# A hash-masked attention followed by an MLP: fp16 transposes, exponentials as the stationary side, and the MLP of one batch woven into the attention of the next

## Chip, cores, metric

The kernel runs on one core of a Trainium2 chip. The metric is the device time of one execution in microseconds (us), the median of several runs. All runs that are compared here are fast (within 1.5% of the fastest run of the same kernel) unless a sentence says otherwise; where some runs of a kernel counted as slow, the median given is that of the fast ones and their number is said. Times inside a kernel come from the trace of one profiled execution, whose span is about 2 us shorter than the device time.

A ratio given with an interval is the mean time of one kernel's fast runs over the mean time of the other kernel's fast runs of the same rounds, so it is not quite the ratio of the medians that are quoted next to it. The experiments ran on four different chips; on each the kernel before took between 423.1 and 423.9 us in the median, so the ratios to it can be compared across chips.

## The reference

Four batches of 8 heads, 768 positions, head dimension 64. Each query and key gets a 6-bit hash (signs of a projection); a query attends only to keys of the same hash. The heads are put side by side (512 columns), and each token goes through an MLP with 2048 hidden units and the activation h cos(h).

```python
q_bits = (np.einsum('bhsd,dk->bhsk', q, proj) > 0)          # k likewise
mask = q_bucket[:, :, :, None] == k_bucket[:, :, None, :]
scores = scale * np.matmul(q, k.transpose(0, 1, 3, 2))
scores = np.where(mask, scores, -1000000000.0)
attn = softmax(scores)                                        # shortened here
x = np.matmul(attn, v).transpose(0, 2, 1, 3).reshape(3072, 512)
h = x @ w_in                                                  # 512 x 2048
out = (h * np.cos(h)) @ w_out                                 # 2048 x 512
```

## The kernel before

Both kernels use the same trick for the mask: the six bits, as +0.5 or -0.5, are appended to the 64 rows of q and k, so that one matmul of 70 rows gives score plus a large bonus for equal hashes, and the exponential of anything else is practically zero. All heads are done first, then all of the MLP. For one head (cuts marked with `...`):

```python
# q and k side by side, [128 positions, 128]: fp32 transposes on TensorE
for t in range(SB):
    nc.tensor.matmul(out=psum_t[:, t*P:(t+1)*P], lhsT=qk_nat[:, t, :], rhs=ident,
                     is_transpose=True, ...)                              # L142
nc.vector.tensor_copy(out=qk_f32, in_=psum_t)                             # L151
for c0, c1 in ((0, 512), (512, 768)):                                     # the hash, fp32
    nc.tensor.matmul(out=psum_t[0:38, c0:c1], lhsT=projx2, rhs=qk_f32[:, c0:c1], ...)  # L159
nc.vector.tensor_scalar(out=q_ext[D:KEXT, :], in0=psum_t[0:NBITS, :], ...)             # L166
...
for jt in range(SB):                                      # 6 steps of 128 keys
    # scores transposed: keys on the partitions, 768 queries along the row
    nc.tensor.matmul(out=st_ps[:, c0:c1], lhsT=k_ext[:, jt*P:(jt+1)*P],
                     rhs=q_ext[:, c0:c1], ...)            # L221, 512 and 256 columns
    nc.scalar.activation(out=pt_sb[:, 0:S], in_=st_ps, func=Exp, ...)     # L229
    # V (and 64 columns of ones) stationary, the exponentials move
    nc.tensor.matmul(out=out_ps[:, c0:c1], lhsT=v_ext[:, jt, :],
                     rhs=pt_sb[:, c0:c1], ...)            # L210, 512 and 257 columns
nc.vector.tensor_scalar(out=numpair[b][t][r0:r0+D, :], in0=out_ps[0:D, 0:S], ...)      # L267
nc.scalar.copy(out=denpair[b][t][r0:r0+D, :], in_=out_ps[D:P, 0:S])                    # L271
```

After the last head each batch is normalised (logarithm and exponential of the denominators on ScalarE, L292 and L298, product on VectorE, L304), and the MLP runs in six chunks of 512 tokens: L321 is the first layer, L329 the sine, L337 the product, L353 and L364 the second layer.

The softmax here doesn't subtract the row's maximum and nothing guards it: scores larger than these inputs give would overflow.

## Time and profile before

| | before |
|---|---|
| time, median | 422.88 us |
| start to first steady score | 16.8 us |
| attention, 32 heads | 223 us; 7.08 us from head to head in the steady part |
| seam to the MLP | 9 us |
| MLP | 168 us |

The first lines of the page: busy time of TensorE, and the busy share in tenths in 40 slices of the span.

```profile
PE 384.4 (91%) x1856; PEld 176.4 (42%) x1856; DVE 243.1 (58%) x352; ACT 306.9 (73%) x389; POOL 37.9 (9%) x58
PE   4889999999999999999999739999999999999996
ACT  1478787878787878787878998968788781660831
```

TensorE (PE) is the busy engine in both stages; the dip in the middle of its row is the seam. The table of windows gives the stages (busy us and number of instructions of each engine, then granted TensorE clock, DMA share, GB/s).

```profile
core 0: us, PE busy (x) PEld busy (x) DVE busy (x) ACT busy (x) POOL busy (x), PEclk, DMA share, GB/s
16.80:240.00 223.20, 207.46 (x1063) 97.45 (x1063) 154.42 (x214) 185.17 (x221) 29.25 (x39) 1.00 0.53 76
240.00:249.00 9.00, 0.54 (x3) 0.25 (x3) 2.39 (x5) 8.90 (x11) 0.00 (x0) 0.65 0.00 0
249.00:417.00 168.00, 167.89 (x768) 75.33 (x767) 78.94 (x114) 109.26 (x156) 0.00 (x0) 0.99 0.10 37
```

In the second of these stretches ScalarE (ACT) is busy for 8.9 of 9 us, most of it with the normalisation of batch 0, and TensorE is idle. The waits name it (engine, tile, line, releaser, total us, times, longest):

```profile
PE h_ps L321 <- DVE xT_97 L304: 8.3, 1, 8.3
```

The groups of instructions give the kinds of matmul (count, then busy us and mean ns of one, then idle time before):

```profile
L221 PE MATMUL st_ps<-q_ext,k_ext 70*128 70x512 bf16 x192 | 71.9, 383 | 3.6 <-ACT pt_buf_161 L229 1.0 <-ACT pt_buf_165 L229 0.3 <-ACT pt_buf_163 L229 0.3
L142 PE MATMUL psum_t<-ident,qk_nat 128*128 128x128 f32 x192 | 36.5, 277 | 6.8 <-DMA qk_nat<-in_k_dram 4.8 <-issue 2.1
L210 PEld LDWEIGHTS <-v_ext_71 128*128 128x128 f16 x132 | 12.9, 98 | 6.3 <-issue 0.6
```

The mean of 383 ns is the latency of one matmul, not what it takes out of the stream. Matmuls overlap, so the difference between the starts of neighbours is the number to use: 216 ns for 512 columns, 109 ns for 256, 109 ns for an fp32 transpose of 128. A weight load (PEld) of 98 ns is always hidden behind such a matmul here: each of the 1856 matmuls has its own load, and those of 512 and 256 columns still start 216 and 109 ns before their neighbour in the median. How waiting in a chain costs time inside a head is seen in the timeline (start, duration, engine, line, in brackets the idle time before and who ended it):

```profile
100.31 0.96 DVE L151 COPY qk_f_969<-psum_t 128x768 f32<-128x768 f32 x1
101.32 1.05 PE L159 MATMUL psum_t<-qk_f_969,projx_63 128*38 128x512 f32 x2 [0.40 <-DVE qk_f_969 L151]
```

The hash reads the copy that VectorE makes of the transposed block, and starts at 101.32 us, 0.05 us after the end of that copy. The block is copied out of PSUM, where both kernels put the results of TensorE. What is called a bank below is a stretch of 512 fp32 columns of a PSUM tile; the tiles of the changed kernel have eight of them.

### The profile page before, as it was taken

To read this page: it belongs to the slowest core of one execution; us is meant where nothing else is said; L and a number is where in the kernel's file an instruction comes from. 1 tells how busy PE (TensorE), PEld (TensorE's weight loads), DVE (VectorE), ACT (ScalarE), POOL (GpSimd) and SP (SyncE) were. 2 spreads that over 40 slices of the span, in tenths; PEclk is the share of its full clock that TensorE was granted. 3 is DMA by queue.
4 is the path that set the end of the run, shared out by engine and by line. 5 is a ranking of instruction groups with operands and counts; after the bars stand their busy time and mean duration, and the time that the engine had idled before them with its cause. 6 is when DMAs were issued, how large, how long until landed. Compare 5 with 4: busy or idle time off the path is not lost.

```text
span 420.9 us, 5065 instructions
## 1 busy us (share of the span) xinstructions
PE 384.4 (91%) x1856; PEld 176.4 (42%) x1856; DVE 243.1 (58%) x352; ACT 306.9 (73%) x389; POOL 37.9 (9%) x58
## 2 busy tenths in 40 slices
PE   4889999999999999999999739999999999999996
PEld 1334444444444444444343314444444444444442
DVE  3576676767686768676867337348355372360630
ACT  1478787878787878787878998968788781660831
POOL 6260101010101010111100000000000000000000
PEclk9899999999999999999999959999999999999999
DMA  9999363636363636363611000020020110200202
GB/s 171 206 198 180 62 81 57 83 55 87 52 90 50 93 47 95 48 94 48 93 11 9 0 2 1 0 101 0 0 101 1 51 51 0 101 0 2 100 25 75
DMA packets 81784, 26.54 MB, mean 63 GB/s; under 512 B 76128, under 2 KB 78176, under 8 KB 81760
## 3 DMA queue, kind: packets, MB, share of 16 engines
q1 hardware_dynamic: 51440, 18.29, 18.6%
q0 software_dynamic: 27968, 7.34, 17.1%
q10 hardware_dynamic: 2352, 0.59, 0.7%
q8 instruction: 14, 0.23, 0.2%
q14 instruction: 10, 0.08, 0.1%
HBM read 27.27 MB, written 6.29 MB: 80 GB/s over the span
## 4 chain that ended last, share of the span: by engine, by line
PE 71%; ACT 18%; DVE 5%; issue 4%; DMA 1%; ACTq 0%
PE h_ps L321 20%; PE out_ps L210 10%; PE st_ps L221 9%; PE psum_t L159 8%; ACT pt_buf_167 L229 6%; PE psum_t L142 5%; ACT pt_buf_165 L229 3%; ACT pt_buf_163 L229 3%; ACT pt_buf_161 L229 1%; DMA qk_nat<-in_k_dram 1%; PE o_ps_3374 L353 1%; PE o_ps_3149 L364 1%; PE o_ps_3147 L364 1%; PE o_ps_2925 L364 1%; PE o_ps_2923 L364 1%
## 5 line engine op out<-in xcount | busy, mean ns | idle before, releaser
L337 DVE TENSOR_TENSOR g_sb<-h_ps,cos_sb 128x512 f16<-128x512 f32 x96 | 65.3, 691 | 58.5 <-ACT cos_sb L329 58.3
L221 PE MATMUL st_ps<-q_ext,k_ext 70*128 70x512 bf16 (+1 forms) x384 | 94.2, 328 | 3.6 <-ACT pt_buf_161 L229 1.0
L329 ACT ACTIVATE cos_sb<-h_ps,cos_bias 128x512 f16<-128x512 f32 x96 | 64.8, 692 | 13.9 <-PE h_ps L321 13.4
L221 PEld LDWEIGHTS <-k_ext 70*128 70x128 bf16 x384 | 34.5, 97 | 63.7 <-issue 46.9
L229 ACT ACTIVATE pt_buf_161<-st_ps,exp_bias 128x768 f16<-128x768 f32 x32 | 28.8, 901 | 41.9 <-PE st_ps L221 41.9
L364 PEld LDWEIGHTS <-g_sb 128*128 128x128 f16 x320 | 31.2, 98 | 37.8
L321 PE MATMUL h_ps<-xT_97,win_77 128*128 128x512 f16 x96 | 36.9, 386 | 8.3 <-DVE xT_97 L304 8.3
L142 PE MATMUL psum_t<-ident,qk_nat 128*128 128x128 f32 x192 | 36.5, 277 | 6.8 <-DMA qk_nat<-in_k_dram 4.8
L255 DVE TENSOR_SCALAR vsum_sb<-out_ps 128x1 f32<-128x1 f32 x32 | 5.1, 158 | 62.8 <-PE out_ps L210 62.8
L321 PE MATMUL h_ps<-xT_98,win_78 128*128 128x512 f16 x96 | 36.8, 385 | 0.0
L321 PE MATMUL h_ps<-xT_99,win_79 128*128 128x512 f16 x96 | 36.6, 384 | 0.0
L321 PE MATMUL h_ps<-xT_100,win_80 128*128 128x512 f16 x96 | 36.6, 384 | 0.0
L166 DVE TENSOR_SCALAR q_ext<-psum_t 6x768 bf16<-6x768 f32 x32 | 30.4, 949 | 5.3 <-PE psum_t L159 4.3
L142 PEld LDWEIGHTS psum_t<-ident,qk_nat 128*128 128x128 f32 x192 | 24.1, 142 | 18.5 <-issue 7.6
L229 ACT ACTIVATE pt_buf_165<-st_ps,exp_bias 128x768 f16<-128x768 f32 x32 | 28.8, 901 | 3.4 <-PE st_ps L221 2.7
L229 ACT ACTIVATE pt_buf_167<-st_ps,exp_bias 128x768 f16<-128x768 f32 x32 | 28.8, 901 | 3.1 <-PE st_ps L221 0.7
L174 DVE TENSOR_SCALAR k_ext<-psum_t 6x768 bf16<-6x768 f32 x32 | 30.5, 952 | 0.4
L229 ACT ACTIVATE pt_buf_171<-st_ps,exp_bias 128x768 f16<-128x768 f32 x32 | 28.9, 902 | 0.0
L229 ACT ACTIVATE pt_buf_163<-st_ps,exp_bias 128x768 f16<-128x768 f32 x32 | 28.6, 893 | 0.0
L229 ACT ACTIVATE pt_buf_169<-st_ps,exp_bias 128x768 f16<-128x768 f32 x32 | 28.6, 893 | 0.0
L321 PEld LDWEIGHTS <-win_77 128*128 128x128 f16 x96 | 9.5, 99 | 19.9 <-issue 8.8
L210 PEld LDWEIGHTS <-v_ext_73 128*128 128x128 f16 x132 | 12.8, 97 | 7.7 <-issue 1.7
(721 smaller groups left out, 603.1 us busy)
## 6 DMA issues: line engine op xcount, KB each, us to landing
qk_nat<-in_q_dram SPq DMA_DIRECT2D x32, 192.0 KB, 2.8
out_dram<-o_sb SPq DMA_DIRECT2D x24, 256.0 KB, 2.0
qk_nat<-in_k_dram SPq DMA_DIRECT2D x29, 192.0 KB, 3.9
v_ext_71<-in_v_dram POOLq DMA_DIRECT2D x11, 96.0 KB, 4.6
v_ext_73<-in_v_dram POOLq DMA_DIRECT2D x11, 96.0 KB, 4.3
v_ext_75<-in_v_dram POOLq DMA_DIRECT2D x10, 96.0 KB, 4.3
qk_nat<-in_k_dram ACTq DMA_DIRECT2D x3, 192.0 KB, 4.9
win_77<-in_moe_w_in_dram POOLq DMA_DIRECT2D x1, 512.0 KB, 8.9
```

Source lines behind the costliest of these rows:

```text
L142: nc.tensor.matmul(out=psum_t[:, t * P:(t + 1) * P], lhsT=qk_nat[:, t, :], rhs=ident, is_transpose=True, start=t in (0, 4), stop=t in (3, 5),)
L159: nc.tensor.matmul(out=psum_t[0:38, c0:c1], lhsT=projx2, rhs=qk_f32[:, c0:c1], start=True, stop=True,)
L166: nc.vector.tensor_scalar(out=q_ext[D:KEXT, :], in0=psum_t[0:NBITS, :], scalar1=0.0, scalar2=0.5, op0=mybir.AluOpType.is_gt, op1=mybir.Alu ...
L174: nc.vector.tensor_scalar(out=k_ext[D:KEXT, :], in0=psum_t[32:32 + NBITS, :], scalar1=0.0, scalar2=0.5, op0=mybir.AluOpType.is_gt, op1=myb ...
L210: nc.tensor.matmul(out=out_ps[:, c0:c1], lhsT=v_ext[:, jt, :], rhs=pt_sb[:, c0:c1], start=(jt == 0), stop=(jt == SB - 1),)
L221: nc.tensor.matmul(out=st_ps[:, c0:c1], lhsT=k_ext[:, jt * P:(jt + 1) * P], rhs=q_ext[:, c0:c1], start=True, stop=True,)
L229: nc.scalar.activation(out=pt_sb[:, 0:S], in_=st_ps, func=mybir.ActivationFunctionType.Exp, bias=exp_bias, scale=EXP_SCALE,)
L255: nc.vector.tensor_scalar(out=vsum_sb[:, 0:1], in0=out_ps[:, S:S + 1], scalar1=DELTA, scalar2=None, op0=mybir.AluOpType.mult,)
L321: nc.tensor.matmul(out=h_ps, lhsT=win_t[ft][:, ff * P:(ff + 1) * P], rhs=xT[ft][:, tok0:tok0 + TOK_CHUNK], start=(ft == 0), stop=(ft == NF ...
L329: nc.scalar.activation(out=cos_sb, in_=h_ps, func=mybir.ActivationFunctionType.Sin, bias=cos_bias, scale=1.0,)
L337: nc.vector.tensor_tensor(out=g_sb, in0=h_ps, in1=cos_sb, op=mybir.AluOpType.mult)
L364: nc.tensor.matmul(out=o_ps[tt], lhsT=g_tiles[ff][:, tt * P:(tt + 1) * P], rhs=wout_t[ff], start=(ff == 0), stop=(ff == NFF - 1),)
```

## The change

The intent: shorten what TensorE does outside the scores, take the normalisation and the copies off ScalarE, and let the second layer of one batch fill TensorE's waits in the attention of the next. In its parts:

- q and k are cast to fp16 on GpSimd and transposed in fp16. The hash no longer needs the transposed fp32 data: VectorE transposes 32 x 32 blocks in SBUF, and four column groups of TensorE hash the four q and k of a pair of heads. The bits reach their rows by a VectorE shuffle and a small DMA.
- The exponentials are the stationary side and V (64 columns and a column of ones) moves. The sums come out with queries on the partitions, so the denominator is one column and the normalisation two short VectorE instructions. The result is transposed for the MLP by a transposing DMA.
- After head 8, 16 and 24 the first layer of the batch that is complete runs, and its second layer is handed out two matmuls per step during the heads that follow.

The diff, cut to its core:

```diff
-    psum_t = att_ps.tile([P, SB * P], FP32, ...)          # and st_ps x2, out_ps
+    s_ps = [psp.tile([P, 2, 512], FP32, name=f"s_ps{i}") for i in range(2)]
+    av_ps = psp.tile([P, 2, 512], FP32, name="av_ps")
+    m_ps = psp.tile([P, 2, 512], FP32, name="m_ps")
...
+    def free_bank():
+        return 1 - state["m"]
+    def hash_mm(pr):
+        hb = m_ps[:, free_bank(), 0:T * 32]
+        for c in range(2):
+            for j in range(4):
+                nc.tensor.matmul(out=hb[32*j:32*j+32, :]..., lhsT=projblk[:, c, :],
+                                 rhs=blk[pr][j % 2][:, j // 2, :, c, :], ...)      # L147
+    def transposes(pr, hh):
+        tr = m_ps[:, free_bank(), :].bitcast(FP16)
+        for t in range(T):
+            nc.tensor.transpose(out=tr[:, t*P:(t+1)*P], in_=n16..., identity=ident16)  # L176
+        nc.vector.tensor_copy(out=ops[pr][0:D, 2*hh, :], in_=tr[0:D, 0:S])         # L180
+        nc.vector.tensor_copy(out=ops[pr][0:D, 2*hh+1, :], in_=tr[D:P, 0:S])       # L181
+    def av(h, jt):
+        bank = av_ps[:, h % 2, :]
+        if jt == 0: ...  # matmul with delta_w starts the sums                     # L205
+        for qt in range(T):
+            nc.tensor.matmul(out=bank[:, qt*W:qt*W+D+1], lhsT=pt[:, qt*P:(qt+1)*P],
+                             rhs=vx_bufs[pr % 3][:, hh, jt, 0:D+1], ...)           # L212
+    def norm(h):
+        nc.vector.reciprocal(out=rc, in_=bank[:, :, D])                            # L223
+        nc.vector.tensor_tensor(out=xn..., in0=bank[:, :, 0:D], in1=rc..., op=mult) # L226
+    def l2_mm(item, last=False):
+        if ff == 0:
+            state["m"] = 1 - state["m"]
+        o_ps = m_ps[:, state["m"], :]
+        nc.tensor.matmul(out=o_ps, lhsT=g[:, qt*P:(qt+1)*P], rhs=wout_t[ff], ...)  # L266
+        if ff == NFF - 1:
+            nc.vector.tensor_copy(out=ob, in_=o_ps)                                # L271
...
+            for jt in range(T):
+                score(h, jt)                                                       # L190, exp L196
+                ...  av of two steps before; norm and transposing DMA at the end of a head
+                fill(2)                          # two second-layer matmuls
+                ...  at fixed steps: loads, casts, hash, transposes of the next pair
+            if h in (8, 16, 24):
+                ...  drain
+                l1(b - 1)                        # first layer, L243; sine L249, product L252
+                l2q.extend(l2_items(b - 1))
```

## The prediction

> **What bounds the kernel now.** Two stages follow each other. In the table of windows the attention runs from 17 to 240 us, one head per 7.08 us, TensorE 93% and ScalarE 83% busy; the MLP from 249 to 417 us with TensorE busy throughout. Between them TensorE waits 8.3 us for the normalisation on ScalarE (the waits). From starts in the timeline, a matmul of 512 columns takes 216 ns of the stream, one of 256 takes 109. Per head: scores 1.97, attention times V 1.97, fp32 transposes 0.65, fp32 hash about 1.4: 6.0 of 7.08 us; the rest is waiting in chains (transpose, VectorE copy, hash, exponential). The MLP, 6 x 128 x 216 ns = 166 us, is at its floor. TensorE bounds, with 1.1 us lost per head, 9 us at the seam and 17 us at the start.
>
> **TensorE after.** MLP 166 us and scores 63 us: the same columns. Attention times V: 6 matmuls of 65 columns per step instead of 769 columns in two, each with its own 128-column weight load. The columns alone would be 27 ns; a weight load is recorded at 97 ns here, always hidden behind 109 ns or more, so this trace doesn't show the pace of small pairs. [...] I estimate 60 ns (30 to 100): 1152 x 60 = 69 us against 63 now: no gain. Delta matmuls add 5 us. Transposes: 12 of about 55 ns per pair of heads, not 109: 11 us, not 21. Hash: 8 fp32 matmuls of 192 columns in four column groups: 2.6 us per pair if serial, 0.7 if they overlap: 11 to 41 us, now 45. Sum 325 to 355 us, now about 357.
>
> **Other engines.** ScalarE loses the denominator copies (32 x 0.80), the normalisation (about 38 us) and the output copies (24 x 0.59); it keeps 192 exponentials of 0.78 us (start to start) and 64 sines of about 0.8, some 200 us. VectorE: about 9.5 us per pair. Loads become 1.5 KB rows instead of 256 B.
>
> **Schedule.** Start about 15 us: hash, shuffle and a DMA of the bits precede the first score. Heads 0 to 8 have no MLP to weave in: about 5.8 us each, 52. First MLP layer 4 x 21. Heads 9 to 31 with 12 second-layer matmuls each: about 8.0 us each, 184, TensorE-bound. Last second layer 21, output 2.5, four seams (tables, buffers, transposing DMA) about 3 each. Sum 15 + 52 + 84 + 184 + 21 + 2.5 + 12 = about 370; I say 368 us, range 342 to 400. Chances: faster by over 2% 0.94, within 2% 0.04, slower 0.02.
>
> **What would show it.** Woven heads with TensorE near 95% busy and steps of about 1.15 us; starts of 65-column matmuls 60 ns apart; heads 0 to 8 at about 5.8 us; ScalarE total near 240 us; four seam gaps of 2 to 4 us.
>
> **What would make it wrong.** Small pairs at 100 ns add about 40 us, at 30 ns take 30 off. Hash groups that don't overlap: up to 20 us. Transposing DMAs slower than the 4 us before a first layer. GpSimd casts and weight DMA issue (about 0.55 us each, with waits of 2 us) too late for the transposes in heads 0 to 8. An in-order queue holding an urgent instruction behind a waiting one.

One sentence is cut out of the recorded text, where the mark stands: a figure for the pace of small pairs that no trace of this case shows. The 60 ns after it leaned on that figure in part and is left as the author's estimate; it lies between two numbers of the trace of before, 27 ns (65 columns at 216 ns per 512) and the 97 ns of a recorded weight load. TensorE's work adds up to 325 to 355 us, and the stages to 15 + 52 + 84 + 184 + 21 + 2.5 + 12 = 370.5 us. The other paces of the forecast are estimates from the same trace: 128 fp16 columns at 216 ns per 512 are 54 ns (for the transposes it says 55), and the MLP's "floor" is its 768 matmuls at the measured 216 ns.

## The result, and the profile after

| | before | after |
|---|---|---|
| time, median | 422.88 us | 385.25 us (383.24 to 387.56) |
| TensorE busy | 384.4 us | 323.9 us |
| ScalarE busy | 306.9 us | 238.1 us |
| TensorE idle, share of the span | 9% | 16% |

The ratio is 0.91 (0.906 to 0.914). The page after, and its row of granted clock:

```profile
PE 323.9 (84%) x2912; PEld 187.6 (49%) x2912; DVE 190.6 (50%) x407; ACT 238.1 (62%) x267; POOL 128.5 (33%) x154
PE   0299878899798888999798888899798979999884
ACT  2067988877676666766666676676776658567000
PEclk9999999999899999999899999999899999999998
```

TensorE lost 60 us of busy time but the kernel only 38 us: TensorE now has 8s and 7s where it had 9s. The stages in the table of windows (first the start, heads 0 to 8, one first layer with its seam, heads 9 to 16 woven, the last second layer):

```profile
0.00:18.80 18.80, 3.12 (x28) 1.78 (x28) 8.68 (x32) 2.53 (x4) 15.42 (x24) 1.00 0.41 127
18.80:75.40 56.60, 48.58 (x577) 31.28 (x578) 30.42 (x87) 45.33 (x55) 44.74 (x56) 1.00 0.89 197
75.40:98.20 22.80, 20.82 (x129) 12.44 (x128) 16.28 (x19) 15.28 (x18) 1.60 (x3) 1.00 0.17 55
98.20:164.10 65.90, 57.88 (x601) 33.18 (x601) 30.37 (x79) 45.68 (x50) 27.23 (x30) 0.97 0.34 89
354.10:383.60 29.50, 21.48 (x96) 9.17 (x94) 5.70 (x8) 0.90 (x1) 0.00 (x0) 0.97 0.14 54
```

The clock of 1.00 in the first two rows is no reading up to 33.5 us: this trace has no clock record before that, and the view shows 1.00 there all the same. By starts it was half: up to 32 us the score matmuls of 512 columns start 381 to 427 ns before their neighbour where nothing holds them up, and from 34 us on 215 to 227 ns. The seam with the logarithms is gone, as intended; what is left of it are three waits of TensorE of 2.0 us, each after a first layer. At the end of each (98.3, 187.1 and 275.8 us) the clock records have 3.4 us at half clock. The groups that answer to those shown of before:

```profile
L212 PE MATMUL av_ps<-vx,pt 128*128 128x65 f16 x1152 | 67.5, 195 | 0.7 <-ACT pt L196 0.7
L212 PEld LDWEIGHTS <-pt 128*128 128x128 f16 x1152 | 61.8, 99 | 29.9 <-issue 6.5 <-ACT pt L196 0.9
L176 PE MATMUL m_ps<-ident,n 128*128 128x128 f16 x192 | 17.2, 230 | 9.7 <-POOL n L111 5.3 <-DVE ob L271 3.9 <-DVE bt L154 0.5
```

By differences of starts, the 65-column matmuls follow each other every 29 ns, although each has its own weight load that is still recorded at 99 ns. Attention times V therefore takes 1152 x 29 ns = 33 us of the stream at full clock, not the 69 us that I had estimated. The fp16 transposes start 56 ns apart (107 ns at 5.4 us, before the first clock record). The sixteen instructions of a hash (eight fp32 matmuls, each two instructions) take 0.8 us together; in the timeline four of them start within 0.02 us, so the column groups do overlap:

```profile
110.09 0.35 PE L147 MATMUL m_ps<-blkq,projblk 128*32 128x192 f32 x1
110.09 0.35 PE L147 MATMUL m_ps<-blkk,projblk 128*32 128x192 f32 x1
110.10 0.35 PE L147 MATMUL m_ps<-blkq,projblk 128*32 128x192 f32 x1
110.11 0.35 PE L147 MATMUL m_ps<-blkk,projblk 128*32 128x192 f32 x1
110.27 0.33 PE L147 MATMUL m_ps<-blkq,projblk 128*32 128x192 f32 x1
```

So the stream of TensorE became shorter than predicted, and yet the time is 17 us above the prediction. The waits say where to look:

```profile
PEld L205 <- DVE xn L226: 7.9, 15, 0.7
PE m_ps L266 <- DVE ops L181: 13.4, 19, 0.7
PE m_ps L266 <- DVE ob L271: 5.5, 11, 0.8
```

The figures of such waits are too small, because the end of a matmul in the profile is its modelled latency, about 170 ns after its place in the stream is free (386 ns recorded for 512 columns, 216 by starts). I worked out the waits again from starts: for each matmul, the difference to the next start less the usual difference for its kind. In the first woven batch (98.2 to 164.1 us) that gives 9.3 us of waits of second-layer matmuls and transposes for VectorE's copies L181 and L271, and 2.0 us of the delta matmul for the normalisation; in all three woven batches 25.2 and 5.7 us. In the timeline of a woven step:

```profile
113.73 0.50 PE L176 MATMUL m_ps<-ident,n 128*128 128x128 f16 x6
114.27 0.55 DVE L180 COPY ops<-m_ps 64x768 f16<-64x768 f16 x1 [1.69 <-PE m_ps L176]
114.40 0.35 PE L212 MATMUL av_ps<-vx,pt 128*128 128x65 f16 x6
114.83 0.56 DVE L181 COPY ops<-m_ps 64x768 f16<-64x768 f16 x1
115.45 0.59 PE L266 MATMUL m_ps<-wout,g 128*128 128x512 f16 x2 [0.70 <-DVE ops L181]
```

The second-layer matmul at 115.45 waits until the copy of the transposes has ended. But the transposes stand in the other bank of `m_ps` (that is what `free_bank` is for), and nothing that this matmul needs depends on the copy. The last second layer, where nothing else runs, shows the same with the output copy:

```profile
357.55 0.69 DVE L271 COPY ob<-m_ps 128x512 f32<-128x512 f32 x1 [1.56 <-PE m_ps L266]
358.30 1.02 PE L266 MATMUL m_ps<-wout,g 128*128 128x512 f16 x4 [0.78 <-DVE ob L271]
```

Two accumulators are there to let the next sixteen matmuls run during this copy, and they don't: 0.94 us is lost by starts, five times, 4.7 us. The instruction list of the built program agrees: 46 of the 384 second-layer matmuls carry a wait for VectorE.

Finally the chain of waits at the start (start, duration, what):

```profile
2.13 6.52 DMA proj<-in_proj_dram
8.78 0.32 DVE projblk L299
9.83 0.58 DVE blkq L135
12.85 1.55 PE m_ps L147 x16
16.92 1.85 DMA ops<-br
```

VectorE starts its instructions in the order of the program here. The four small copies that build the hash matrix wait for a tiny load that lands at 8.65 us, and behind them stand the block transposes of data that had landed at about 4.1 us.

### The profile page after: what moved, and what is told of

It reads as the page before. It is cut to its first block, busy times and chain, and to the rows that moved or that the text cites. A ratio compares the mean times of both kernels' runs of the same rounds, so it can differ in the third digit from the quotient of the medians.

```text
span 383.6 us, 7314 instructions
## 1 busy us (share of the span) xinstructions
PE 323.9 (84%) x2912; PEld 187.6 (49%) x2912; DVE 190.6 (50%) x407; ACT 238.1 (62%) x267; POOL 128.5 (33%) x154
## 4 chain that ended last, share of the span: by engine, by line
PE 69%; DVE 16%; DMA 6%; ACT 4%; issue 4%; SPq 0%; POOL 0%; ACTq 0%; DVEq 0%; POOLq 0%
PE m_ps L266 21%; PE s_ps L243 15%; PE s_ps L190 12%; PE av_ps L243 7%; PE av_ps L212 6%; DVE ob L271 4%; PE m_ps L147 4%; ACT pt L196 3%; DMA ops<-br 3%; DVE xn L226 3%; DVE ops L181 3%; PE m_ps L176 3%; DVE ops L180 2%; PE av_ps L205 2%; DMA proj<-in_proj_dram 2%
## 5 line engine op out<-in xcount | busy, mean ns | idle before, releaser
L196 ACT ACTIVATE pt<-s_ps,exp_bias 128x768 f16<-128x768 f32 x192 | 169.0, 900 | 80.0 <-PE s_ps L190 75.4
L266 PE MATMUL m_ps<-wout,g 128*128 128x512 f16 x384 | 109.0, 386 | 19.3 <-DVE ops L181 13.4
L190 PE MATMUL s_ps<-ops 70*128 70x512 f16 (+1 forms) x384 | 100.4, 345 | 15.2 <-DVE g L252 5.9
L212 PEld LDWEIGHTS <-pt 128*128 128x128 f16 x1152 | 61.8, 99 | 29.9 <-issue 6.5
L212 PE MATMUL av_ps<-vx,pt 128*128 128x65 f16 x1152 | 67.5, 195 | 0.7 <-ACT pt L196 0.7
L243 PEld LDWEIGHTS <-win 128*128 128x128 f16 x512 | 49.9, 98 | 33.1 <-issue 0.3
L243 PE MATMUL s_ps<-xT,win 128*128 128x384 f16 x352 | 61.3, 326 | 0.1
L190 PEld LDWEIGHTS <-ops 70*128 70x128 f16 x384 | 35.2, 101 | 51.5 <-issue 22.5
L249 ACT ACTIVATE cos<-s_ps,cos_bias 128x768 f16<-128x768 f32 x44 | 39.6, 900 | 22.3 <-PE s_ps L243 22.3
L252 DVE TENSOR_TENSOR g<-s_ps,cos 128x768 f16<-128x768 f32 x44 | 42.1, 957 | 18.0 <-ACT cos L249 18.0
L111 POOL TENSOR_SCALAR n<-natk 128x384 f16<-128x384 f32 x32 | 37.4, 1168 | 3.6 <-DMA natk<-in_k_dram 1.2
L271 DVE COPY ob<-m_ps 128x512 f32<-128x512 f32 x24 | 16.5, 688 | 34.0 <-PE m_ps L266 34.0
```

What stands on the lines that cost most here:

```text
L111: nc.gpsimd.tensor_scalar(out=o_, in0=i_, scalar1=sc, scalar2=None, op0=ALU.mult)
L190: nc.tensor.matmul(out=sp[:, c, 0:c1 - c0], lhsT=ops[pr][0:KEXT, 2 * hh + 1, jt * P:(jt + 1) * P], rhs=ops[pr][0:KEXT, 2 * hh, c0:c1], sta ...
L196: nc.scalar.activation(out=pt, in_=sp.rearrange("p c n -> p (c n)")[:, 0:S], func=ACTF.Exp, bias=exp_bias, scale=EXP_SCALE)
L212: nc.tensor.matmul(out=bank[:, qt * W:qt * W + D + 1], lhsT=pt[:, qt * P:(qt + 1) * P], rhs=vx_bufs[pr % 3][:, hh, jt, 0:D + 1], start=Fal ...
L243: nc.tensor.matmul(out=hp[:, c, 0:C2], lhsT=win_t[ft][:, ff * P:(ff + 1) * P], rhs=xT[(b, ft)][:, 3 * c:3 * c + 3, :], start=(ft == 0), st ...
L249: nc.scalar.activation(out=cos, in_=hp[:, :, 0:C2], func=ACTF.Sin, bias=cos_bias, scale=1.0)
```

## The experiments

The theory after the result (A): the changed kernel waits for the wrong bank, because the waits are derived for whole tiles and each pair of banks is one tile. The main rival (B): two banks are truly too few for three uses.

### e1: one tile per bank for m_ps

```diff
-    m_ps = psp.tile([P, 2, 512], FP32, name="m_ps")
+    m_ps = [psp.tile([P, 512], FP32, name=f"m_ps{i}") for i in range(2)]
```

(and `m_ps[:, bank, :]` becomes `m_ps[bank]`.)

> Edit: the two-bank PSUM tile m_ps (second-layer accumulator, hash, transposes) becomes two tiles of one bank each; nothing else. Theory A (a wait on the wrong bank: the changed kernel's TensorE waits, before a matmul into one bank, for VectorE's copy out of the other bank, because both banks are one tile): the waits of the second-layer matmuls for the ops and ob copies, by the difference of starts about 9.3 us per woven batch and 4.2 us in the last second layer, go: about 358 to 364 us, against 385. Rival B (true reuse: two banks are too few for three uses, and the copies are of the bank that is needed next): no change, 382 to 388 us. In the last second layer A expects matmul groups 216 ns apart, B the gap of 0.8 us every 16 matmuls.

Measured: 361.34 us (four fast runs of six; 363.54 over all six), ratio to the kernel before 0.854 (0.850 to 0.859), where the changed kernel had 0.910. Now 12 of the 384 second-layer matmuls carry a wait for VectorE. The end of the kernel in the timeline:

```profile
336.66 8.58 PE L266 MATMUL m_ps<-wout,g 128*128 128x512 f16 x39
339.45 0.69 DVE L271 COPY ob<-m_ps 128x512 f32<-128x512 f32 x1 [1.56 <-PE m_ps L266]
```

39 matmuls run through without a gap while VectorE copies. A holds and B falls: the same eight banks suffice when each is its own tile. The fp16 view (`bitcast`) in which the transposes write their bank is not the cause either: the output copies of the last second layer have none and were waited for all the same.

### e2: the same for av_ps as well

```diff
-    av_ps = psp.tile([P, 2, 512], FP32, name="av_ps")
+    av_ps = [psp.tile([P, 512], FP32, name=f"av_ps{i}") for i in range(2)]
```

(the first layer, which uses `av_ps` as its third buffer, gets two sines and two products of 384 columns there.)

> Edit: as e1, and av_ps also becomes two tiles of one bank; every third first-layer step then needs two sines and two products of 384 columns. Theory A: the delta matmul no longer waits for the normalisation of the head before (0.28 us per head, 2 to 3 us per batch): 5 to 9 us less than e1, so about 352 to 357 us. Rival B: as e1 or 1 to 2 us slower for the extra instructions.

Measured: 351.79 us, ratio 0.830 (0.827 to 0.833): 10 us less than the fast runs of e1, a little more than the 5 to 9 expected. In the two profiled runs 1.7 us of the 10 lie before head 9, and about 2 us in head 9, where e1's trace has the half clock for 6.8 us and e2's for 3.4; what is left is near the 5.7 us of waits that had been counted. The step that answers to the one shown above:

```profile
114.93 0.50 PE L176 MATMUL m_ps<-ident,n 128*128 128x128 f16 x6
115.60 0.34 PE L212 MATMUL av_ps<-vx,pt 128*128 128x65 f16 x6
115.78 0.59 PE L272 MATMUL m_ps<-wout,g 128*128 128x512 f16 x2
116.03 0.56 DVE L181 COPY ops<-m_ps 64x768 f16<-64x768 f16 x1
```

The second-layer matmuls (now line 272) start 0.18 us after the 65-column ones and before the copy L181 has even begun. The two splits together are worth 0.080 of the time of before, 34 us; the waits that I had worked out from starts in the changed kernel were 25.2 + 5.7 + 4.7 = 36 us.

### e3: the start, VectorE's order

```diff
-        for b_ in range(4):
-            nc.vector.tensor_copy(out=projblk[32*b_:...], in_=proj4[...])
         ...
         transposes(0, 0)
+        for b_ in range(4):
+            nc.vector.tensor_copy(out=projblk[32*b_:...], in_=proj4[...])
         hash_mm(0)
```

> Edit: in the changed kernel the four small VectorE copies that build the hash matrix move from before the block transposes to just before the hash. Theory C (in-order VectorE: the copies wait until 8.7 us for the small projection load, and hold the block transposes whose data landed at 4.1 us): the first score starts near 16 us instead of 18.8, so 382 us, 3 less than 385. Rival D (the start is bound by the loads and by the DMA of the bits): no change.

Measured: 385.5 us (four fast runs of six, 383.04 to 387.31; the two slow ones reach 394.81), ratio 0.910 (0.906 to 0.914): no gain in the total. The chain at the start did move as C said:

```profile
2.15 5.93 DMA proj<-in_proj_dram
9.53 1.55 PE m_ps L147 x16
13.63 1.85 DMA ops<-br
```

The first exponential began at 16.4 instead of 19.7 us. In the profiled run head 9 began at 97.6 instead of 99.5 us, so part of the gain was lost by then, and the rest went in head 17, which took 10.5 instead of 7.6 us while the granted clock was half for 10.2 us instead of 3.4. The cause of the lost time at the start is shown; that it is worth 3 us in the total is not.

### e4: filling at the seam

```diff
                 l2q.extend(l2_items(b - 1))
+                fill(10)
```

> Edit: after each woven first layer, 10 second-layer matmuls are issued before the next head's first score. Theory E: they cover the 2 us in which TensorE waits at each of three seams for the last sine and product, and the 3.4 us at half clock that follow go too: 3 x (2 + up to 1.7), so 375 to 379 us. Rival F: the later heads only run out of filling sooner and the gain is handed back, or the waits for the wrong bank take it: 383 to 386 us.

Measured: 394.23 us (five fast runs of six), ratio 0.930 (0.927 to 0.934), 9 us slower, worse than either theory said. The three stretches from the first exponential of head 8, 16 and 24 over the seam to that of the next head took 30.6, 32.6 and 33.6 us against 30.6, 32.3 and 32.3, with ten more matmuls (2.2 us) in them; the seven woven heads of the first batch took 59.3 against 56.4 us (with a half-clock stretch of 3.4 us in them, and 5.5 us instead of 2.0 us of waits for the normalisation), those of the second 57.8 against 56.4. E's total is refuted. Why it got slower was open at this point: waits for the wrong bank, or filling that ran out.

### e5: 127 columns of weights

```diff
-                out=bank[:, qt * W:qt * W + D + 1],
-                lhsT=pt[:, qt * P:(qt + 1) * P],
+                out=bank[0:127, qt * W:qt * W + D + 1],
+                lhsT=pt[:, qt * P:(qt + 1) * P - 1],
```

(on top of e1; the result is wrong, relative error 0.09.) The question is whether the 29 ns between small matmuls depend on the 128 columns of the stationary side.

> Edit: e1 with 127 instead of 128 columns of the exponentials as the stationary side (one query row in 128 gets no sum: wrong result on purpose). Theory G [...]: starts 53 ns or more apart, 1152 of them, so 20 to 36 us slower than e1's 363.5: 380 to 398 us. Rival H (small pairs are limited by their 65 moving columns, 27 ns, and weight loads always hide): 29 ns still, 361 to 367 us.

Measured: 412.65 us, ratio 0.976 (0.973 to 0.978), 51 us slower than the fast runs of e1. At full clock the small matmuls now start 59 ns apart in the median, twice the 29 ns:

```profile
L212 PEld LDWEIGHTS <-pt 128*127 128x127 f16 x1152 | 116.4, 167 | 33.3 <-issue 18.9
L212 PE MATMUL av_ps<-vx,pt 128*127 128x65 f16 x1152 | 112.3, 241 | 0.0
```

G's figure holds for the pace: 53 ns or more was an estimate, near what 127 columns take at 216 ns per 512 (53.6). The total rose by more than 1152 x 30 ns = 35 us; in this run the small matmuls of heads 0 to 8 ran at half clock (starts 107 ns apart, for instance at 40 us), so its lines above mix both clocks. From head 9 to the end, e5's profiled run took 283.3 us and e1's 260.2: 23 us more, where 23 heads x 36 pairs x 30 ns = 25 us. The other 29 us lie before head 9, where e1 has the full clock from about 25 us on but for short stretches, and e5 not before 106 us. The mean of a recorded weight load rose from 99 ns in the changed kernel to 167 ns, but this mean mixes both clocks too. A count other than 127 was not run.

### e6: e2 with the filling of e4

> Edit: e2 (both PSUM tiles split) plus the 10 second-layer matmuls at each seam that cost 8 us in e4. Theory F (in e4 the seam gain was taken back by waits for the wrong bank, because the new phase of accumulators against copies met more of them): now 3 to 8 us below e2's 351.8, 344 to 349 us. Rival I (filling early only leaves later heads unfilled, whatever the banks): 351 to 355 us.

Measured: 357.35 us (five fast runs of six, mean 358.8), ratio 0.848 (0.844 to 0.852), 7 to 8 us slower than e2 by means and ratios. F falls: without the shared tiles the filling at the seam still does harm. Rival I is nearer: by its account a head that comes after the queue has run dry (16 and 24) leaves TensorE idle, and before a first layer nothing is left to do while the transposing DMA runs. Of this the trace shows the second part: TensorE waits 3.2 us for that DMA at three first layers, 2.2 us of it at the last; e2 has no such wait, while e4 too has a gap of 2.6 us before its last first layer. In the profiled run that last first layer took 20.8 us from first to last sine instead of 19.5, with a half-clock stretch at its beginning. I also predicted too little loss here (351 to 355 us).

### e7: e2 with constant-data matmuls at the start and an early projection

```diff
-            nc.gpsimd.dma_start(out=proj4[:, c, :], ...)       # after load(0)
+            nc.scalar.dma_start(out=proj4[:, c, :], ...)       # before load(0)
+        heat(9)                  # matmuls of 512 columns on constant data
         transposes(0, 0)
+        heat(4)
         hash_mm(0)
         ...
+        heat(20)
```

> Edit: e2 plus the projection loaded first on ScalarE's queue, and 33 matmuls on constant data while TensorE would idle before the first score. Theory J (heads 0 to 2 take 8.3, 6.8 and 7.4 us because TensorE still runs at half clock until 25 to 40 us, where a score takes 0.64 instead of 0.33 us and two score buffers no longer hide it; and the start is held by the projection): first exponential at 13 to 15 us instead of 19.2, heads 0 to 2 at 5 to 5.8 us, together 338 to 344 us against 351.8. Rival K (ScalarE and the DMA of the bits set these heads): only the start gains, 346 to 349 us.

Measured: 351.56 us, ratio 0.831 (0.829 to 0.832), the same as e2; both theories missed. The projection's two DMAs on ScalarE's queue pushed the loads of k behind others, so that k was ready at 8.3 us and the first exponential still began at 18.95 us. The last twenty constant-data matmuls also stood in the way: they ran from 14.27 to 18.59 us, and the first score followed at once. Heads 0 and 1 did become faster (5.4 and 5.6 us instead of 8.3 and 6.8), and later heads slower (7.1 us in head 4, where e2 had 5.8); head 9 began at 98.7 us, in e2 at 98.8.

### e8: no weaving

```diff
                 l2q.extend(l2_items(b - 1))
+                fill(1000)
```

> Edit: the changed kernel with all 96 second-layer matmuls issued right after the first layer instead of woven into the next heads. Theory A (woven heads lose most of the gain to waits for the wrong bank): heads 9 to 31 fall from 8.2 to about 5.6 us, and three second layers of 20.7 + 4.2 us come to stand alone: about 397 us, so weaving is worth only 8 to 17 us of the 60 us of matmuls woven. Rival: weaving hides most of the 60 us already: 425 to 445 us.

Measured: 404.75 us, ratio 0.956 (0.952 to 0.960), a little above what A expected (397) and far below the rival's 425. Heads 9 to 15 fell from 8.1 us in the mean to 5.7. So weaving is worth 19.5 us in the changed kernel (404.75 - 385.25; A had said 8 to 17), although 276 matmuls of 216 ns, 60 us, are woven: it hides only part of them. That the waits for the wrong bank take the rest is not shown by this run alone.

### e9: output weights later

```diff
-                if h < 8 and u == 4:      # in heads 0, 2: w_in; in heads 4, 6: w_out
+                if h < 4 and u == 4:      # in heads 0, 2: w_in
+                    ...
+                if h == 8 and u == 4:     # all of w_out
```

> Edit: e2, with all 16 loads of the output weights issued in head 8 instead of in heads 4 and 6 (they are first used after the first layer, 21 us later). Theory M (heads 0 to 8 end at 73 to 75 us in every version, whatever their start and clock, because the DMA engines are about 90% busy there, at some 200 GB/s, with loads and weights): 4.2 MB less in that stretch, so head 8 ends at 66 to 69 us and the whole takes 344 to 348 us against e2's 351.8. Rival N (ScalarE, GpSimd and the clock set these heads): head 8 ends at 72 to 75 us, 350 to 354 us.

Measured: 356.58 us (three fast runs of six, 354.95 to 359.62; the slow ones reach 362.78), about 5 us slower than e2. The ratio of 0.848 (0.844 to 0.853) doesn't fit these three, whose mean over that of the kernel before is 0.843; it is near that of all six. The last exponential of head 8 began at 71.2 us, against 73.4 in e2: a little in M's direction, nearer to N. Even this can't be put down to the weights, because in these traces e9 has the full clock from about 26 us on and e2 only from 40. And the weights came in the way of something urgent:

```profile
PE s_ps L243 <- DMA xT<-xn: 4.3, 1, 4.3
```

The transposing DMA that the first first layer needs took 9.5 us to land while they were loading, where the one before the last first layer took 2.7. e2 has no such wait there.

### e10 to e12: putting the parts together

e10 is e9 with the start of e3, constant-data matmuls in the idle places of the start, `fill(10)` at the seams, and the later filling thinned so that it lasts:

```diff
-                fill(2)
+                s_ = h * T + jt
+                thin = s_ % 7 in (2, 5) if h >= 24 else s_ % 5 == 4
+                fill(1 if thin else 2)
```

> Edit: e9 plus the start of e3 (hash-matrix copies behind the block transposes), constant-data matmuls while TensorE would idle before the first score, 10 second-layer matmuls at each seam, and the later filling thinned (one instead of two in every fifth step) so that it lasts to the end of the batch. Theory M with J and E: start 3 us, heads 0 to 8 near 5.2 us each (head 8 ends at 61 to 64 us), seams 2 us each: 334 to 340 us. If the thinning is wrong (rival I again): 342 to 348 us.

Measured: 349.03 us, ratio 0.823 (0.821 to 0.825): neither range. From head 9 to the end it took 246.3 us, e2 251.9, so thinned filling together with `fill(10)` does pay, where `fill(10)` alone had cost (e6): TensorE's gaps of 2.3 us after the first layers are gone, and the half clock that follows them in e2. Thinning alone was not run. But head 9 began at 101.0 us because of the late weights.

> Edit: e10 without the constant-data matmuls. Theory J (half clock in the first heads costs about 1.5 us in each of heads 0 to 2): 3 to 6 us slower than e10. Rival M alone (DMA sets the pace, the clock doesn't matter): within 1 us of e10.

Measured (e10 without `heat`): 350.66 us, ratio 0.827 (0.825 to 0.830), 1.6 us slower than e10. Only head 0 differs much (7.2 against 5.4 us). This is less than J said, but not a test of three heads at half clock: by starts e11 had the full clock from 22.2 us on, within head 0.

> Edit: e10 with the output weights loaded in heads 4 and 6 again, as in the changed kernel: so e2 plus the start, the constant-data matmuls, the filling at the seams and its thinning. In e9 and e10 the late weights held up the transposing DMA before the first first layer (4.4 us of wait) and gave the gain of heads 0 to 8 back; from head 9 to the end e10 took 246 us against e2's 252. If that is the whole account: head 9 starts at 96 to 99 us as in e2 and the total is 342 to 346 us. If the heads before are slower for the earlier start: 347 to 350 us.

Measured (e10 with the weights back in heads 4 and 6): 340.92 us (339.25 to 341.67), ratio 0.8045 (0.802 to 0.807), the best version of all and correct; it is about 12% below the changed kernel (0.8045 / 0.910 = 0.884). The page:

```profile
PE 314.4 (93%) x2945; PEld 187.3 (55%) x2945; DVE 190.5 (56%) x428; ACT 237.6 (70%) x287; POOL 128.5 (38%) x154
PE   6788798899989999899988999899989999999995
```

Head 9 began at 93.5 us and the rest took 246.3 us. The last exponential of head 8 began at 68.1 us, in e10, with 4.2 MB of weights less in that stretch, at 68.4: so theory M falls in the form tested, that those megabytes set the pace of heads 0 to 8. With e3's expected 3 us and the seams' filling, both of which gave nothing or did harm alone, this version gained 11 us over e2.

## Why the prediction was right or wrong

The direction and the range were right (385.25 us in 342 to 400); the middle, 368, was 17 us too low. It was also nearer than its reasoning deserves, because two terms were wrong in opposite directions.

- **The MLP, scores, transposes and hash: right.** A first layer takes 20.8 us (predicted 21), fp16 transposes start 56 ns apart (predicted 55), and the hash takes 0.8 us per pair of heads (0.7 if the groups overlap). The four column groups work side by side in this trace: four starts in 0.02 us, each of these instructions recorded with 0.33 to 0.35 us. ScalarE's total was predicted near 240 us and is 238.1.
- **The pace of small pairs: mis-sized.** The step "I estimate 60 ns (30 to 100)" measured 29 ns, below its own range. 1152 x 31 ns = 36 us of TensorE work, about 26 us of it in woven heads (23 of 32), was counted that doesn't exist, and "no gain there" is wrong: 33 us instead of 63. The estimate lay between the 27 ns of the columns alone and the 97 ns of a recorded weight load; measured is the lower of the two, nearly, although each small matmul has its own load, recorded at 99 ns. The trace of before didn't show that loads hide behind so short a matmul, as the prediction says. What the traces do show is about 0.42 to 0.45 ns per column for 16-bit matmuls at full clock: 216 ns at 512 columns, 109 at 256, 56 at 128 and 29 at 65. In e5, with 127 columns of the stationary side instead of 128, the small matmuls start 59 ns apart.
- **Woven heads "TensorE near 95% busy", "TensorE-bound": this step failed.** TensorE was busy 57.9 of 65.9 us (88%) in the first woven batch by the profile, and about 50 us (75%) by starts. A usual step took 0.94 us, not 1.15, but a head still took 8.2 us (8.0 predicted), because steps with a copy in them waited for it. What stands in its place is the wait of a matmul for a copy out of the other bank, since two banks were one tile: about 31 us in the woven heads. e1 and e2 show it, by splitting the shared tiles and nothing else but some sines and products (in the first woven batch of e2 1.1 us of such waits is left, for a copy out of the bank that is needed). I had read the line with `free_bank` and taken it that the banks were independent. The list of what could go wrong had "an in-order queue holding an urgent instruction", not a wait that needn't be there.
- **The last second layer and output: 23.5 predicted, 29.5 measured.** 4.7 us are the same wait, five times.
- **The start: 15 predicted, 18.8 measured.** The mechanism was on the list (an in-order queue). e3 shows it: the first exponential came 3.3 us earlier.
- **Heads 0 to 8: 5.8 us predicted, 6.3 measured (56.6 / 9).** In part settled by the traces. Heads 0 and 1 took 8.3 and 6.8 us, and by its starts TensorE ran at half clock until about 33 us; in e10 and e12, where constant-data matmuls ran before head 0, they took 5.4 and 4.9 to 5.1 us (e10's view has a clock of 0.83 for 10 to 20 us and of 1.00 for 20 to 30 us). The difference, about 4.7 us, is as large as the whole miss. A second thing holds up single later heads, here and in e2, e6, e9, e10 and e12: on the chain that ended last, two DMAs of the bits took 5.25 and 5.72 us (at 40.3 and 51.5 us), where the first took 1.85, and e12 has one of 6.35 us before head 4. Why these land late was not tested: they follow the loads of the next pair on the same queue, and the DMA engines are 89% busy in this stretch.
- **Seams: 12 predicted, 9.4 measured** (three windows of 22.8 us and one of 24.2, less 20.8 each). The transposing DMA was in time at the first three seams, as hoped, and not in e9.

Added up: start +3.8, heads 0 to 8 +4.6, woven heads +2 (about -26 for the pace against about +31 for the waits, the rest small), first layers -0.8, end +6, seams -2.6: +13. The prediction's own sum was 370.5 us, which makes 383.6, the span of the profiled run.

What stays open: why single DMAs of the bits in heads 0 to 8 take three times as long as the first; and how the loss from filling at the seams divides between the dry queue and the waits for the transposing DMA. The shared tiles had little part in it: by ratios the same edit costs 8.6 us with them (e4) and 7.8 us without (e6).

## What to carry to other kernels

Give every PSUM bank that is used by turns its own tile, and look in the trace for a matmul that waits for a copy out of a bank it doesn't write: here that was 34 of 385 us, nearly as much as the whole change had gained. Before trusting an estimate of small matmuls, measure the difference of starts, and be wary of an fp16 stationary side of less than 128 columns (with 127 the small matmuls here started 59 ns apart instead of 29; no other count was run). Filling work is a stock: spending it at one place takes it from another, and filling the seams paid only when the rest was thinned to last until the end of the batch.
